# B's factor moved into C, B turned by DMA transposes, denominators between v's products

## The chip, the cores and the metric

One core of one Trainium2 chip runs the kernel. The metric is device microseconds of one execution. TensorE multiplies (PE in the profile, PEld its weight loads), VectorE (DVE) does elementwise work and reductions, ScalarE (ACT) copies, scales and exponentials, GpSimd (POOL) a few fills, and SyncE (SP) issues nearly all DMAs, in order.

## What is computed

Two unrelated parts share the launch, each on an input of 2048 x 448 (bf16), and their outputs are put side by side.

```python
# A: a complex diagonal state space, state of 448
Lam_bar = jnp.exp(dt * Lam)
B_bar = ((Lam_bar - 1.0) / Lam)[:, None] * Bmat
Bu = jnp.einsum("bld,pd->blp", x + 0j, B_bar)
# h[t] = Lam_bar * h[t-1] + Bu[t]
y = 2.0 * jnp.einsum("blp,dp->bld", hseq, Cmat).real + x * Dskip
# B: attention, 16 heads of 28; each position sees 8 keys, 2 apart, looking back
qkv = x @ wqkv
logits = q . k[pos - 2*w] * scale      # w = 0..7; -1e9 before the start
out = (softmax(logits) weighted v) @ wo
```

The factor g = (Lam_bar - 1)/Lam stands at each state, between B and C, and commutes with the recurrence, which is diagonal.

## The kernel before, in words

**Part B** first. The input is turned to `xT`, products on TensorE with half-height operands (64 rows) give q, k and v. The method `Ctx.lanes` (L88) writes TensorE's order by hand: it runs two lanes, the upper and lower 64 rows, one product of each per step, and chains the products (L83). The list `weave` puts other work in at given steps: the steps of `qk` (L282) multiply q by shifted k on VectorE (L295, L299) and sum on TensorE (L306); then come `turn` (step 157, L772: the matrix `mats["g"]` and the first softmax's transposes and maxima, L330 and L332), the two `expo` calls (steps 160 and 164: one product L337 that subtracts the maxima, one exponential on ScalarE, L339), and `prepare` (step 200, that is, when the lanes are done; L777). `prepare` makes two power matrices, B's products and `norm` (L343: eight products that sum the exponentials, L345, then the reciprocal L348 and the weights L349 on VectorE). v's products are evicted by ScalarE to `vd` (L239), and copies between partitions fill its halo (`halo`, L223).

After that `pv` (L375) weights v: for each of two halves of the positions and two groups of four, eight products (L389) and seven sums (L392) on VectorE, each 128 x 1792. The result is turned by a DMA transpose (L404; the last by TensorE, L411) and multiplied with wo (L420).

**Part A** runs on TensorE and ScalarE under those products. The state is in 7 blocks of 64 complex numbers, each a block of 128 rows (real over imaginary). The matrices of powers of Lam_bar are made by `mat` (L587, L599) from small numbers in `Scat`, on VectorE, at places given by `put` (L793) between the steps of `pv`. B is loaded by `load_bc` (L461) in its natural layout to `bX`. `setup_b` (L601) multiplies it by the factor's matrix, which also turns it: 28 products (L607), evicted by ScalarE into `Bcat` with 14 casts (two for each block, L609 and L610). Level 1 (`level1`, L637) multiplies `Bcat` by the input `xaT` (L643) for four interleaved positions b = 0..3, adding the power times the position before (L647), evicted by ScalarE (L650, L652). `scan` (L655) doubles over chunks (L673, L676), `ends` (L678) makes the states at chunk ends `G`, and `correct` (L695) adds to the others on VectorE (L700). `setup_c` (L615) turns C with 28 transposes on TensorE (L621), evicted by ScalarE in 7 copies, behind the first scan. `y` (L706) multiplies the states by C (L715) and adds the skip by a diagonal matrix `Dg` (L572, ScalarE; its numbers come from `skip`, L564).

**Order.** The lanes and what they weave are chained on TensorE. The rest is laid out per engine when the kernel is built, by a planner that goes by priority and its own estimates; each engine then takes its instructions in that order, and waits in place. Tiles with the same tag share memory, so `oT` waits for `bX` to be read, and `Ccat` for the weights `wn`. Level 1 has four PSUM buffers ("mm"), the corrections two ("pt"). SyncE's queue at the start: part B's input and weights, B (`load_bc`), A's input in eight DMA transposes (`load_x`, L475), zeros for the halo, wo, C (`load_c`), D, then the halo copies.

Of the kernel before, what the change touches and what calls it, by code (L numbers as in the profile page):

```python
# [11 lines left out]
ALU = mybir.AluOpType  # L12
AX = mybir.AxisListType
f32 = mybir.dt.float32
bf16 = mybir.dt.bfloat16

S = 2048
D = 448
T = 16
NCH = 128  # L20
KT = 4
KP = 112
KA = 128
# [10 lines left out]
NM = 7  # L34
MP = 8
PL = 64
# [7 lines left out]
NPW = len(KPOW)  # L44
# [3 lines left out]
class Ctx:  # L48
# [4 lines left out]
    def consts(self):  # L53
        nc, pool = self.nc, self.pool
        self.ident = pool.tile([NCH, NCH], bf16, name="ident")
        nc.gpsimd.memset(self.ident[:], 0.0)
        nc.gpsimd.affine_select(out=self.ident[:], in_=self.ident[:], compare_op=ALU.not_equal, fill=1.0,
                                base=0, pattern=[[-1, NCH]], channel_multiplier=1)
        self.nident = pool.tile([NCH, NCH], bf16, name="nident")
        nc.gpsimd.memset(self.nident[:], 0.0)  # L60
        nc.gpsimd.affine_select(out=self.nident[:], in_=self.nident[:], compare_op=ALU.not_equal, fill=-1.0,
                                base=0, pattern=[[-1, NCH]], channel_multiplier=1)

        self.spot, self.spot2 = (pool.tile([1, 1], f32, name=f"spot{i}") for i in range(2))
        self.wz = pool.tile([NCH, 4 * NCH], bf16, name="wz")
        nc.vector.memset(self.wz[:], 0.0)
# [364 lines left out]
class PartA:  # L431
# [7 lines left out]
    def consts(self):  # L439
        self.kv = self.pool.tile([NCH, NPW, NM], f32, name="kv")  # L440
        for i, kk in enumerate(KPOW):
            self.nc.gpsimd.memset(self.kv[:, i, :], float(kk))
        self.Bcat = self.pool.tile([KA, KT, NM, NCH], bf16, name="Bcat")
        self.nc.vector.memset(self.Bcat[0:KA - PL, KT - 1], 0.0)
        self.Scat = self.pool.tile([NCH, NPW + 1, 2, MP], bf16, name="Scat")
        self.nc.vector.memset(self.Scat[:], 0.0)

# [11 lines left out]
        nc.sync.dma_start(self.drow[KT - 1:KT], self.A_Dskip[D - KA:D].unsqueeze(0))  # L459

    def load_bc(self):  # L461
        nc, pool = self.nc, self.pool
        self.bX = pool.tile([NCH, NM, D], bf16, name="bX", tag="bX")
        nc.sync.dma_start(self.bX[0:PL], self.A_Bre.rearrange("(m p) d -> p m d", p=PL))
        nc.sync.dma_start(self.bX[PL:NCH], self.A_Bim.rearrange("(m p) d -> p m d", p=PL))

    def load_c(self):
        nc = self.nc
# [43 lines left out]
    def powers(self, sm, big, karg, ang, kf, angr, ex, turned):  # L512
        nc, V, lre, lim = self.nc, self.nc.vector, self.lre, self.lim
        self.cx.order(V.tensor_scalar(kf[:], ang[:], 1.0 / TWO_PI, MAGIC, op0=ALU.mult, op1=ALU.add).ins,
                      turned["V"], "NoSync")
        V.tensor_scalar(kf[:], kf[:], MAGIC, None, op0=ALU.subtract)
        C1 = 6.28125
        C2 = 1.9353071795864769e-03
        V.scalar_tensor_tensor(angr[:], kf[:], -C1, ang[:], op0=ALU.mult, op1=ALU.add)
        reduced = self.reduced = V.scalar_tensor_tensor(angr[:], kf[:], -C2, angr[:], op0=ALU.mult, op1=ALU.add).ins  # L520
        sn, sh, cs = sm("sn", big), sm("sh", big, "kf"), sm("cs", big, "karg")
        self.cx.order(nc.scalar.activation(sn[:], angr[:], ACT.Sin).ins, turned["A"], "NoSync")
        nc.scalar.activation(sh[:], angr[:], ACT.Sin, scale=0.5)
        den, t0, rden = sm("dn"), sm("t0"), sm("rden")
        for o_, l_ in ((den, lre), (t0, lim)):
            self.cx.order(V.tensor_tensor(o_[:], l_, l_, op=ALU.mult).ins, reduced, "NoSync")
        V.tensor_tensor(den[:], den[:], t0[:], op=ALU.add)
        V.reciprocal(rden[:], den[:])
        V.tensor_scalar(rden[:], rden[:], 2.0, None, op0=ALU.mult)
        pw_im = sm("pw_im", big)  # L530
        V.tensor_tensor(pw_im[:], ex[:], sn[:], op=ALU.mult)
        V.tensor_tensor(cs[:], sh[:], sh[:], op=ALU.mult)
        V.tensor_scalar(cs[:], cs[:], -2.0, 1.0, op0=ALU.mult, op1=ALU.add)
        pw_re = sm("pw_re", big)
        V.tensor_tensor(pw_re[:], ex[:], cs[:], op=ALU.mult)
        Scat = self.Scat
        V.tensor_copy(Scat[0:PL, 0:NPW, 0, 0:NM], pw_re[0:PL])
        V.tensor_scalar(Scat[0:PL, 0:NPW, 1, 0:NM], pw_im[0:PL], -1.0, None, op0=ALU.mult)
        V.tensor_copy(Scat[PL:NCH, 0:NPW, 0, 0:NM], pw_im[PL:NCH])
        V.tensor_copy(Scat[PL:NCH, 0:NPW, 1, 0:NM], pw_re[PL:NCH])  # L540
        self.pw_re, self.pw_im, self.rden = pw_re, pw_im, rden
        self.mats = {}
# [55 lines left out]
            self.mats[key] = t_[:].rearrange("p h q m -> p m (h q)")  # L598
        return self.nc.vector.tensor_tensor(t_[:], in0, in1, op=ALU.mult).ins  # L599

    def setup_b(self, eng):  # L601
        nc, cx = self.nc, self.cx
        def step(i):
            pt, out = cx.ps([KA, KT, NCH], f32, "pt_b"), []
            for k in range(KT):
                c0 = min(k * KA, D - KA)
                out.append(nc.tensor.matmul(pt[:, k, :], lhsT=self.bX[:, i, c0:c0 + KA], rhs=self.mats["g"][:, i, :],  # L607
                                            start=(k == 0), stop=(k == KT - 1), skip_group_check=True).ins)
            cx.ev(eng, self.Bcat[:, 0:KT - 1, i, :], pt[:, 0:KT - 1])  # L609
            cx.ev(eng, self.Bcat[PL:KA, KT - 1, i, :], pt[PL:KA, KT - 1])  # L610
            return out

        return [lambda i=i: step(i) for i in range(NM)]

    def setup_c(self, eng):  # L615
        nc, cx, pool = self.nc, self.cx, self.pool
        self.C = pool.tile([NCH, NM, D], bf16, name="Ccat", tag="wn")
        for m in range(NM):
            pt = cx.ps([NCH, KT, KP], bf16, "pt_c", "pt")
            for a in range(KT):  # L620
                nc.tensor.transpose(pt[:, a, :], self.cn[:, a, m].rearrange("p r q -> p (r q)"), cx.ident[0:KP, 0:KP])  # L621
            cx.ev(eng, self.C[:, m, :].rearrange("p (a q) -> p a q", q=KP), pt[:])

    def alloc_h(self):
        pool = self.pool
# [11 lines left out]
    def level1(self, mh):  # L637
        nc, cx = self.nc, self.cx
        for b in range(4):
            for m in range(*MH[mh]):  # L640
                ps = cx.ps([NCH, 4 * NCH], f32, "l1", "mm")
                for k in range(KT):
                    nc.tensor.matmul(ps[:], lhsT=self.Bcat[:, k, m, :],  # L643
                                     rhs=self.xT[:, b, k, :],
                                     start=(k == 0), stop=(b == 0 and k == KT - 1))
                if b:
                    nc.tensor.matmul(ps[:], lhsT=self.mats[1][:, m, :], rhs=self.h[b - 1][:, m, :],  # L647
                                     start=False, stop=True)
                if b < 3:
                    nc.scalar.copy(self.h[b][:, m, :], ps[:])  # L650
                else:
                    nc.scalar.copy(self.h[b][:, m, :].rearrange("p (a c) -> p a c", a=4),  # L652
                                   ps[:].rearrange("p (c a) -> p a c", a=4))
# [70 lines left out]
def body(ctx: ExitStack, tc: tile.TileContext, A_x, A_Lre, A_Lim, A_Bre, A_Bim, A_Cre, A_Cim, A_logdt, A_Dskip,  # L724
         B_x, B_wqkv, B_wo, out):
    nc = tc.nc
    pool = ctx.enter_context(tc.tile_pool(name="sb", bufs=1))
    psum = ctx.enter_context(tc.tile_pool(name="ps", bufs=1, space=bass.MemoryType.PSUM))
    out_v = out[0].rearrange("(p j) e -> p j e", j=T)
    cx = Ctx(tc, pool, psum)  # L730
    b = PartB(cx, B_x, B_wqkv, B_wo, out_v[:, :, D:2 * D])
    a = PartA(cx, A_x, A_Lre, A_Lim, A_Bre, A_Bim, A_Cre, A_Cim, A_logdt, A_Dskip, out[0].rearrange("(n b) e -> n b e", b=4)[:, :, 0:D])
# [14 lines left out]
    b.load_w(2 * D, 2 * D, D, nc.sync)  # L747
    a.load_bc()
    a.load_x()
    b.zero_halo(b.vd)  # L750
    b.load_wo()
    a.load_c()
# [9 lines left out]
    def later():  # L762
        powers(b.turned)
        b.mix_w(a.reduced)
        a.params_g()
        return ()

    values = [b.proj(j, "A") for j in (*range(HJ, T), *range(HJ))]
    qk, soft = b.qk(0) + b.qk(1), {}
    weave = [(5, turns[2:] + [later])] + [(s_, [f]) for s_, f in zip(WEAVE, qk)]  # L770
# [5 lines left out]

    def prepare():  # L777
        a.mats_behind([0, 3], b.maxima)
        fs = mats_b[:1] + soft[1][0][4:] + mats_b[1:]
        return [ins for f in fs for ins in f()]  # L780

    mats_b = a.setup_b("A")
    weave += [(157, [turn])] + [(160 + 4 * i, [lambda i=i: soft[1][0][2 + i]()]) for i in range(2)] + [(200, [prepare])]
    cx.lanes([b.proj_t(t0, t1, g, "A") for t0, t1, gs in ((0, 256, (0, 1, 2)), (256, 512, (0, 1, 2)), (0, 512, (4, 5, 6, 3)))
              for g in gs]
             + [b.proj_t(*t, g, "A") for t in parts for g in (0, 1, 2, 4, 5, 6, 3)] + values, weave, 10)
    at1 = soft[1][1]
    b.halo(b.vd, 6, HALO)
    b.halo(b.vd, 0, 6)
    a.skip()  # L790
    fs, at0 = b.softmax(0)

# [20 lines left out]
    for b_, r in itertools.product((3, 0, 1, 2), range(4)):  # L813
        ins = a.y(r, b_)
        if (b_, r) == (1, 3):
            wo[2]()
    turn, out = wo[3]
# [35 lines left out]
```

## Time and profile before

| | |
|---|---|
| median of 3 runs | 151.69 us (151.14 to 152.08) |
| the profiled execution | 151.38 us, its span 149.7 us |
| granted TensorE clock | 1.00 throughout |
| DVE, 50 to 60 us | 7.58 us busy |
| DVE, 60 to 100 us | 10.00 us busy in each 10 us |
| PE, 60 to 70 us | 7.93 us busy |
| PE, 70 to 130 us | 9.79 to 10.00 us busy in each 10 us |
| ACT, 50 to 60 us | 8.08 us busy |

Times in a timeline are microseconds from the start of the span. A timeline line gives start, length (for several instructions from the first's start to the last's end), engine, source line, operation, output and inputs, count, and in brackets the idle time before it and what ended it. In the chain that ended last each piece starts where the one before it ends. "SPq" is an issue on SyncE's queue. A mean of busy time hides stages with different limits, so the text goes by the lines in the order of time.

### The profile page before, as it was taken

What the parts mean: (1) busy time and instruction counts of PE and PEld (TensorE: products, weight loads), DVE (VectorE), ACT (ScalarE), POOL (GpSimd) and SP (SyncE); (2) the same over time, 40 slices, a digit from 0 to 9 for tenths busy, and PEclk for the clock granted to TensorE, in tenths of its full rate; (3) what the DMA queues carried; (4) which work ended last, traced back from release to release, by engine and by line L of the source; (5) the groups of instructions that cost most, each with busy time, mean ns of one, the idle gap of its engine ahead of it and who ended that gap; (6) DMA issues with size and microseconds to landing.
All of it is one profiled execution on the core that took longest, in us unless ns stands there. A gap on an engine that the chain in (4) does not pass through costs nothing.

```text
span 149.7 us, 3246 instructions
## 1 busy us (share of the span) xinstructions
PE 139.7 (93%) x1234; PEld 80.6 (54%) x1240; DVE 131.5 (88%) x178; ACT 90.7 (61%) x200; POOL 8.7 (6%) x84
## 2 busy tenths in 40 slices
PE   6999999999999999589999999999999999899790
PEld 2477744445665675245467555568565655445440
DVE  4368999998999859999999999995999999999821
ACT  3387947886754599964569967779421242245340
POOL 8110100000000200000000000000000000000000
PEclk9999999999999999999999999999999999999999
DMA  4999999993767706000004200045111121832121
GB/s 118 286 176 192 176 242 212 95 211 74 144 115 136 213 4 183 0 0 4 0 0 83 39 4 0 0 118 134 61 64 61 41 87 56 190 120 96 61 92 61
DMA packets 35534, 14.77 MB, mean 99 GB/s; under 512 B 27635, under 2 KB 35137, under 8 KB 35519
## 3 DMA queue, kind: packets, MB, share of 16 engines
q1 hardware_dynamic: 34954, 14.12, 44.2%
q10 hardware_dynamic: 565, 0.46, 0.9%
q8 instruction: 9, 0.15, 0.4%
q14 instruction: 6, 0.05, 0.2%
HBM read 3.85 MB, written 3.67 MB: 50 GB/s over the span
## 4 chain that ended last, share of the span: by engine, by line
PE 68%; DVE 18%; ACT 9%; issue 2%; DMA 1%; DVEq 0%; ACTq 0%
PE qk_ps L121 14%; PE l L643 13%; PE v_ps L121 8%; DVE pvb L392 8%; DVE pvb L389 7%; PE lg L306 6%; PE wo_ps L420 5%; PE warm L71 3%; PE y_ps L715 3%; PE l L647 3%; PE gt L690 3%; PE co L699 3%; ACT h L650 2%; PE l L673 2%; ACT Ccat L144 2%
## 5 line engine op out<-in xcount | busy, mean ns | idle before, releaser
L389 DVE TENSOR_TENSOR pvb<-attn,vd 128x1792 bf16<-128x1792 bf16 (+1 forms) x33 | 34.0, 1052 | 0.0
L643 PE MATMUL l<-xaT,Bcat 128*128 128x512 bf16 x108 | 29.5, 379 | 1.8 <-ACT h L650 1.6
L392 DVE TENSOR_TENSOR pvb<-pvb 128x1792 bf16<-128x1792 bf16 (+1 forms) x29 | 30.3, 1049 | 0.0
L295 DVE TENSOR_TENSOR pr<-q,kT 128x3072 bf16<-128x3072 bf16 x16 | 27.9, 1755 | 1.4 <-PE lg L306 0.7
L121 PE MATMUL qk_ps<-xbT,wqkv_nat 64*128 64x512 bf16 (+1 forms) x189 | 24.8, 353 | 0.1
L718 ACT CAST ya<-y_ps 128x448 bf16<-128x448 f32 x16 | 8.4, 533 | 18.7 <-PE y_ps L715 13.0
L715 PE MATMUL y_ps<-Ccat,h 128*128 128x448 bf16 x84 | 18.0, 353 | 0.0
L643 PEld LDWEIGHTS <-Bcat 128*128 128x128 bf16 x112 | 10.5, 99 | 10.7 <-issue 2.2
L121 PEld LDWEIGHTS <-wqkv_nat 64*128 64x128 bf16 x189 | 11.5, 94 | 8.7 <-issue 2.5
L420 PE MATMUL wo_ps<-wo_p,oT 128*128 128x448 bf16 x64 | 14.7, 352 | 1.0 <-DMA oT<-pvb 1.0
L650 ACT CAST h<-l 128x512 bf16<-128x512 f32 x21 | 12.4, 623 | 4.3 <-PE l L647 4.2
L700 DVE TENSOR_TENSOR h<-co,h 128x512 bf16<-128x512 f32 x21 | 13.2, 685 | 2.0 <-PE gt L690 1.6
L121 PE MATMUL v_ps<-wqkv_nat,xbT 64*128 64x448 bf16 x112 | 13.2, 360 | 0.0
L144 ACT CAST kT<-qk_ps 128x512 bf16<-128x512 f32 (+4 forms) x26 | 10.0, 424 | 3.7 <-PE qk_ps L121 3.6
L144 ACT CAST yb<-wo_ps 128x448 bf16<-128x448 f32 x14 | 7.5, 534 | 6.0 <-PE wo_ps L420 3.1
L144 ACT CAST q<-qk_ps 128x512 bf16<-128x512 f32 (+1 forms) x20 | 9.6, 497 | 1.2 <-PE qk_ps L121 1.1
L144 ACT CAST vd<-v_ps 128x448 bf16<-128x448 f32 x16 | 8.0, 539 | 4.0 <-PE v_ps L121 3.8
L715 PEld LDWEIGHTS <-h 128*128 128x128 bf16 x84 | 7.3, 98 | 5.3
L676 ACT CAST pbuf<-l 128x512 bf16<-128x512 f32 (+2 forms) x21 | 9.1, 439 | 1.5 <-PE l L673 1.5
L306 PE MATMUL lg<-pr,ones 128*32 128x256 bf16 x256 | 9.9, 275 | 0.0
L121 PEld LDWEIGHTS <-xbT 64*128 64x128 bf16 x112 | 7.6, 145 | 3.5 <-issue 1.9
L420 PEld LDWEIGHTS <-oT 128*128 128x128 bf16 x64 | 6.0, 98 | 6.5 <-DMA oT<-pvb 1.4
(137 smaller groups left out, 192.0 us busy)
## 6 DMA issues: line engine op xcount, KB each, us to landing
out_dram<-yb SPq DMA_DIRECT2D x16, 112.0 KB, 2.1
out_dram<-ya SPq DMA_DIRECT2D x16, 112.0 KB, 1.7
vd<-vd SPq DMA_DIRECT2D x1, 784.0 KB, 5.4
wqkv_nat<-in_B_wqkv_dram SPq DMA_DIRECT2D x2, 336.0 KB
vd<-vd SPq DMA_DIRECT2D x1, 588.0 KB
xn<-in_B_x_dram SPq DMA_DIRECT2D x2, 224.0 KB, 3.4
bX<-in_A_B_re_dram SPq DMA_DIRECT2D x1, 392.0 KB, 4.4
bX<-in_A_B_im_dram SPq DMA_DIRECT2D x1, 392.0 KB
```

Source lines behind the costliest of these rows:

```text
L121: ins = mm(g["ps"], lhsT=l_, rhs=r_, start=first, stop=not (g["left"][0] or g["left"][1]), skip_group_check=True).ins
L144: nc.scalar.copy(out, in_)
L295: queued(V.tensor_tensor(pr[:], q[0][:, :, n * qu:n * qu + n].unsqueeze(2).to_broadcast([KA, KT - 1, 4, n]), self.shifted(i, 0, KT - 1, s, ...
L306: out.append(mm(lg[32 * t:32 * t + 32, n * qu:n * qu + n], lhsT=l_, rhs=r_, start=not (s or qu or c), stop=(s == 1 and c == KT - 1), skip_ ...
L389: V.tensor_tensor(t_[:, c0:c1], at[:, w, jl0 + c0:jl0 + c1, :].unsqueeze(2).to_broadcast([NCH, c1 - c0, DH, H]), self.vd[:, off + c0:off + ...
L392: ins = V.tensor_tensor(acc[:, c0:c1], acc[:, c0:c1], t_[:, c0:c1], op=ALU.add).ins
L420: ins = nc.tensor.matmul(ps[:], lhsT=oT[:, 7 * i + 3 * odd + k, :], rhs=self.wo_p[:, odd, k, :], start=(k == 0), stop=(k == KT - 1)).ins
L643: nc.tensor.matmul(ps[:], lhsT=self.Bcat[:, k, m, :], rhs=self.xT[:, b, k, :], start=(k == 0), stop=(b == 0 and k == KT - 1))
L650: nc.scalar.copy(self.h[b][:, m, :], ps[:])
L676: nc.scalar.copy(dst[:, :, PAD:], ps[:])
L700: nc.vector.tensor_tensor(self.h[b][:, m, :], ps[:], self.h[b][:, m, :], op=ALU.add)
L715: out.append(nc.tensor.matmul(ps[:], lhsT=self.state(m, r, b), rhs=self.C[:, m, :], start=False, stop=(m == NM - 1), skip_group_check=True ...
```

## The change

B is loaded in the same natural layout, but padded to 512 columns (the last 64 of the 448 stand behind 64 columns of zeros), in four transfers instead of two, and two DMA transposes (`turn_b`) turn it into `Bcat`, whose two middle dimensions change places. The factor is no longer in it. C is turned by one DMA transpose (`turn_c`), and seven products with the factor's matrix (`setup_c`) give what `y` reads. The signs in `Scat` follow. In `prepare`, at step 167 instead of 200, stand the two power matrices and `norm`; the second `expo` stands at step 162 instead of 164. `setup_b` is gone.

```diff
--- before.py
+++ after.py
@@ -440,8 +440,9 @@
         self.kv = self.pool.tile([NCH, NPW, NM], f32, name="kv")
         for i, kk in enumerate(KPOW):
             self.nc.gpsimd.memset(self.kv[:, i, :], float(kk))
-        self.Bcat = self.pool.tile([KA, KT, NM, NCH], bf16, name="Bcat")
-        self.nc.vector.memset(self.Bcat[0:KA - PL, KT - 1], 0.0)
+        self.Bcat = self.pool.tile([KA, NM, KT, NCH], bf16, name="Bcat")
+        self.bX = self.pool.tile([NCH, NM, KT * KA], bf16, name="bX", tag="bX")
+        self.nc.vector.memset(self.bX[:, :, (KT - 1) * KA:KT * KA - PL], 0.0)
         self.Scat = self.pool.tile([NCH, NPW + 1, 2, MP], bf16, name="Scat")
         self.nc.vector.memset(self.Scat[:], 0.0)
 
@@ -459,10 +460,24 @@
         nc.sync.dma_start(self.drow[KT - 1:KT], self.A_Dskip[D - KA:D].unsqueeze(0))
 
     def load_bc(self):
-        nc, pool = self.nc, self.pool
-        self.bX = pool.tile([NCH, NM, D], bf16, name="bX", tag="bX")
-        nc.sync.dma_start(self.bX[0:PL], self.A_Bre.rearrange("(m p) d -> p m d", p=PL))
-        nc.sync.dma_start(self.bX[PL:NCH], self.A_Bim.rearrange("(m p) d -> p m d", p=PL))
+        n = (KT - 1) * KA
+        for r, src in enumerate((self.A_Bre, self.A_Bim)):
+            v, o_ = src.rearrange("(m p) d -> p m d", p=PL), self.bX[r * PL:(r + 1) * PL]
+            self.nc.sync.dma_start(o_[:, :, 0:n], v[:, :, 0:n])
+            self.nc.sync.dma_start(o_[:, :, KT * KA - PL:], v[:, :, n:])
+
+    def turn_b(self):
+
+        for m0, m1 in ((0, 4), (4, 7)):
+            self.nc.sync.dma_start_transpose(self.Bcat[:, m0:m1].rearrange("p m k c -> p (m k) c"),
+                                             self.bX[:, m0:m1].rearrange("p m d -> p (m d)"))
+
+    def turn_c(self):
+        both = self.pool.tile([NCH, 2, NM * D], bf16, name="Ccat", tag="wn")
+        self.C = both[:, 0].rearrange("p (m d) -> p m d", d=D)
+        self.cT = both[:, 1].rearrange("p (a m q) -> p a m q", a=KT, q=KP)
+        self.nc.sync.dma_start_transpose(both[:, 1].rearrange("p (c q) -> p c q", q=KP),
+                                         self.cn[:].rearrange("p a m r q -> p (a m r q)"))
 
     def load_c(self):
         nc = self.nc
@@ -535,8 +550,8 @@
         V.tensor_tensor(pw_re[:], ex[:], cs[:], op=ALU.mult)
         Scat = self.Scat
         V.tensor_copy(Scat[0:PL, 0:NPW, 0, 0:NM], pw_re[0:PL])
-        V.tensor_scalar(Scat[0:PL, 0:NPW, 1, 0:NM], pw_im[0:PL], -1.0, None, op0=ALU.mult)
-        V.tensor_copy(Scat[PL:NCH, 0:NPW, 0, 0:NM], pw_im[PL:NCH])
+        V.tensor_copy(Scat[0:PL, 0:NPW, 1, 0:NM], pw_im[0:PL])
+        V.tensor_scalar(Scat[PL:NCH, 0:NPW, 0, 0:NM], pw_im[PL:NCH], -1.0, None, op0=ALU.mult)
         V.tensor_copy(Scat[PL:NCH, 0:NPW, 1, 0:NM], pw_re[PL:NCH])
         self.pw_re, self.pw_im, self.rden = pw_re, pw_im, rden
         self.mats = {}
@@ -598,28 +613,12 @@
             self.mats[key] = t_[:].rearrange("p h q m -> p m (h q)")
         return self.nc.vector.tensor_tensor(t_[:], in0, in1, op=ALU.mult).ins
 
-    def setup_b(self, eng):
-        nc, cx = self.nc, self.cx
-        def step(i):
-            pt, out = cx.ps([KA, KT, NCH], f32, "pt_b"), []
-            for k in range(KT):
-                c0 = min(k * KA, D - KA)
-                out.append(nc.tensor.matmul(pt[:, k, :], lhsT=self.bX[:, i, c0:c0 + KA], rhs=self.mats["g"][:, i, :],
-                                            start=(k == 0), stop=(k == KT - 1), skip_group_check=True).ins)
-            cx.ev(eng, self.Bcat[:, 0:KT - 1, i, :], pt[:, 0:KT - 1])
-            cx.ev(eng, self.Bcat[PL:KA, KT - 1, i, :], pt[PL:KA, KT - 1])
-            return out
-
-        return [lambda i=i: step(i) for i in range(NM)]
-
     def setup_c(self, eng):
-        nc, cx, pool = self.nc, self.cx, self.pool
-        self.C = pool.tile([NCH, NM, D], bf16, name="Ccat", tag="wn")
+
         for m in range(NM):
-            pt = cx.ps([NCH, KT, KP], bf16, "pt_c", "pt")
-            for a in range(KT):
-                nc.tensor.transpose(pt[:, a, :], self.cn[:, a, m].rearrange("p r q -> p (r q)"), cx.ident[0:KP, 0:KP])
-            cx.ev(eng, self.C[:, m, :].rearrange("p (a q) -> p a q", q=KP), pt[:])
+            ps = self.cx.ps([NCH, D], f32, "c_ps", "pt")
+            self.nc.tensor.matmul(ps[:], lhsT=self.mats["g"][:, m, :], rhs=self.cT[:, :, m, :], start=True, stop=True)
+            self.cx.ev(eng, self.C[:, m, :], ps[:])
 
     def alloc_h(self):
         pool = self.pool
@@ -640,7 +639,7 @@
             for m in range(*MH[mh]):
                 ps = cx.ps([NCH, 4 * NCH], f32, "l1", "mm")
                 for k in range(KT):
-                    nc.tensor.matmul(ps[:], lhsT=self.Bcat[:, k, m, :],
+                    nc.tensor.matmul(ps[:], lhsT=self.Bcat[:, m, k, :],
                                      rhs=self.xT[:, b, k, :],
                                      start=(k == 0), stop=(b == 0 and k == KT - 1))
                 if b:
@@ -747,6 +746,7 @@
     b.load_w(2 * D, 2 * D, D, nc.sync)
     a.load_bc()
     a.load_x()
+    a.turn_b()
     b.zero_halo(b.vd)
     b.load_wo()
     a.load_c()
@@ -776,17 +776,16 @@
 
     def prepare():
         a.mats_behind([0, 3], b.maxima)
-        fs = mats_b[:1] + soft[1][0][4:] + mats_b[1:]
-        return [ins for f in fs for ins in f()]
-
-    mats_b = a.setup_b("A")
-    weave += [(157, [turn])] + [(160 + 4 * i, [lambda i=i: soft[1][0][2 + i]()]) for i in range(2)] + [(200, [prepare])]
+        return soft[1][0][4]()
+
+    weave += [(157, [turn])] + [(160 + 2 * i, [lambda i=i: soft[1][0][2 + i]()]) for i in range(2)] + [(167, [prepare])]
     cx.lanes([b.proj_t(t0, t1, g, "A") for t0, t1, gs in ((0, 256, (0, 1, 2)), (256, 512, (0, 1, 2)), (0, 512, (4, 5, 6, 3)))
               for g in gs]
              + [b.proj_t(*t, g, "A") for t in parts for g in (0, 1, 2, 4, 5, 6, 3)] + values, weave, 10)
     at1 = soft[1][1]
     b.halo(b.vd, 6, HALO)
     b.halo(b.vd, 0, 6)
+    a.turn_c()
     a.skip()
     fs, at0 = b.softmax(0)
```

## The prediction

> **What bounds the kernel now.** I read the page's busy shares first, then the chain that ended last, then VectorE's timeline over the whole span, and last the timelines of ScalarE, TensorE and SyncE around the lines that the diff touches.
>
> ```profile
> PE 139.7 (93%) x1234; PEld 80.6 (54%) x1240; DVE 131.5 (88%) x178; ACT 90.7 (61%) x200; POOL 8.7 (6%) x84
> ```
>
> Two engines are nearly full, so the share decides nothing; the place of the idle time does. VectorE's timeline (start, length, instruction, idle before it):
>
> ```profile
> 54.81 0.96 DVE L348 RECIPROCAL rec<-den 128x128 bf16<-128x128 f32 x1 [1.73 <-PE den L345]
> ...
> 101.90 1.08 DVE L389 TENSOR_TENSOR pvb<-attn,vd 128x1792 bf16<-128x1792 bf16 x1
> 104.57 1.29 DVE L700 TENSOR_TENSOR h<-co,h 128x512 bf16<-128x512 f32 x2 [1.59 <-PE gt L690]
> 106.14 12.04 DVE L700 TENSOR_TENSOR h<-co,h 128x512 bf16<-128x512 f32 x19 [0.28 <-PE co L699]
> ```
>
> From 54.81 to its last product at about 141.3 VectorE rests only 1.59 and 0.28 us, and before that it waits 1.73 us for the denominators. After it comes a tail of transposes and output of some 8.4 us. So the end moves by what those three rests lose, as long as TensorE keeps up. TensorE's part of the chain, where the change bites:
>
> ```profile
> 52.76 0.32 PE lt L337
> 53.08 0.91 PE v_ps L121 x6
> 53.99 0.33 PE pt_b L607 x4
> 54.32 0.45 PE den L345 x8
> 54.77 1.34 PE pt_b L607 x24
> ...
> 59.49 0.47 ACT Bcat L144
> 60.28 0.28 issue
> 60.55 0.97 ACT Dg L572 x3
> 61.55 0.58 ACT h L650
> ```
>
> The reader sees that B's products hand the chain to ScalarE, which then holds it up to the first eviction of level 1. The same in the timeline of all engines:
>
> ```profile
> 54.79 5.44 ACT L144 CAST Bcat<-pt_b 128x384 bf16<-128x384 f32 x14
> ...
> 60.25 1.28 ACT L572 ACTIVATE Dg<-ident,dsk 128x128 bf16<-128x128 bf16 x4
> 61.55 0.58 ACT L650 CAST h<-l 128x512 bf16<-128x512 f32 x1
> ...
> 62.19 1.02 PE L643 MATMUL l<-xaT,Bcat 128*128 128x512 bf16 x4 [1.60 <-ACT h L650]
> ```
>
> ScalarE takes its instructions in order: 14 evictions of Bcat, 4 of Dg, and only then h. TensorE's four buffers for level 1 are full meanwhile, and the second round (b=1) starts at 62.19. From there TensorE is nearly dense to the first correction product at 104.37, whose result ends VectorE's 1.59 us rest. That links ScalarE's 5.44 us to the end.
>
> **The change part by part.**
>
> *B's products leave.* 24 of them stand between 54.61 and 56.04, 0.06 us each, so 28 are 1.7 us of TensorE; 14 evictions are 5.44 us of ScalarE, in the one stretch where ScalarE leads. Nothing on VectorE leaves but a fill of 0.43 us at 1.23, which a smaller fill replaces, ahead of a rest of 2.3 us: nothing. The sign moved between two small instructions (L538, L539, 0.23 and 0.25 us) costs nothing.
>
> *B's transposes come, on SyncE's queue.* Nearest rows, a transpose between two places on chip and its reader:
>
> ```profile
> 127.26 1.52 SPq L404 DMA_TRANSPOSE oT<-pvb  x1
> ...
> 131.27 3.22 PE L420 MATMUL wo_ps<-wo_p,oT 128*128 128x448 bf16 x16 [0.96 <-DMA oT<-pvb]
> ```
>
> It turns 14 blocks: 1.52 us of the queue and 4.0 us to the reader. B has 16 and 12 blocks: 3.0 us of the queue. The two loads of B become four; the old took 0.76 and 0.62 us to issue, so 1.4 us more. SyncE ended the last transpose of A's input at 32.2; the new ones are issued at about 33.6 to 36.6 and land by 41 to 45 (4 to 8 us, if the second waits for the first). Level 1 reads Bcat at 55, so 10 us cover it. What stands behind on the queue slips by 4.4 us: halo zeros, ten transfers of wo, eight loads of C, two of D, the first halo copy. C's last load goes out before 50.5 and lands (3.8) by 54.3. The first halo goes from 47.14 to 51.5, lands by 57 (5.4) and is first read by the product for w=5, the second of the pair at 66.62. The second halo waits 6.2 us for v's last eviction, so it has slack for 4.4. The 10 us cover all of it; without cover each us would be a us of level 1.
>
> *C.* 28 transposes on TensorE (eight from 77.45 to 77.85, so 0.05 us each, 1.4 us) become 7 products of 448 columns. The row of y's products, seven in 1.49 us with a tail, gives 0.19 us each, 1.3 us. Seven copies of 0.59 us become seven casts like ya's, 0.53 us. Nothing either way. The transpose of C is 28 blocks, so twice the row above: 3.0 us of queue and at most 8 us to land. It stands behind the second halo (55.5 to 56.4, both halves out) and needs the weights' buffer, free when v's products end near 55; it lands by 65. The products for C stand at 77.45 now, near 75 then. Behind it on the queue is the transpose at 79.59, with 15 us of cover.
>
> *Denominators.* They were called after all of v's products; now at step 167. Counting the lanes' two products a step, the last step is 167 with a single product, which agrees with the trace (8 products between the two L337, 7 behind the second). The second L337 moves from step 164 to 162. New order, from the first L337's end at 51.85: 4 products 0.46, L337 0.32, 10 products 1.14, then the denominators. The 0.33 us of the chain's four B products less 4 x 0.06 leaves 0.09 for the change of product shape, and 0.45 follow: end 54.31 for 54.77. The exponentials that they read must be there: ScalarE started the second at 53.47 behind two evictions of v whose groups end in steps 162 and 163, now behind it. It can start at 52.7 and end by 53.4, before 53.77. So the reciprocal starts 0.4 us earlier, at 54.4. Ends of this: 0 (if ScalarE keeps its order) and 0.86 (if the products start at 53.4); the rows put it in the middle, and I take 0.4. Queued behind the denominators on TensorE are one product of v, whose eviction ends near 55.4 instead of 54.95 (read by VectorE at 57), and the transposes for softmax.
>
> [...] The row: TensorE's weight loads for L337 show 0.32 us of "issue" behind v's half-height products. [...] The denominators now have such products on both sides, so one pair of changes more. [...]
>
> *TensorE to the first correction.* Denominators end 54.3, one product with its changes 0.6: 54.9. Eight transposes for softmax 0.68, sixteen products of level 1 at 0.215 are 3.44, one L337 0.32: b=1 can start at 59.3, against 62.19. ScalarE has Dg from 56.2 to 57.5 and the first h at 58.0, so it no longer holds. What is late next: L337 for the other softmax needs VectorE's maxima, which end at 59.29 now, 58.9 then; TensorE reaches its place (behind 11 products) at 57.95, so up to 0.95 us is lost again. The gain is 2.0 to 2.9 us. Later, the scan's power 512 comes off VectorE at 83.1, 82.7 then; its products at 85.27 come to 82.4 to 83.3: up to 0.3 us. So the first correction product is at 101.5 to 102.7 instead of 104.37.
>
> *VectorE.* It ends its product at 102.98, then at 102.58, and the correction can follow at 101.7 to 102.9 (0.2 behind its product). The rest of 1.59 us goes, but for 0.3 at the worst. The 0.28 us (wo's products queued ahead of the second pair) I leave in place. TensorE must be earlier at the end too: it rests 0.96 us at 131.27 and 0.87 us at 140.88 there, so 2 us follow.
>
> *Sum.* 0.4 + 1.6 = 2.0 us. The profiled execution took 151.38 us (span 149.7), so 149.4; it lies 0.3 under the median of 151.69, which gives 149.7. I say 149.5.
>
> **The rivals.**
> 1. *The gap stays.* TensorE's order is laid out anew and gives the 2 to 2.9 us back between 59 and 102 (waits for maxima and powers). For it: VectorE is full, and TensorE's margin at the correction is only 0 to 0.9 us. Against: the removed work is in the stretch with 2 us of rest. Then only the 0.4 remains: 151.0, or 151.3 by the median.
> 2. *Slower: TensorE waits for C's transpose.* The new wait is in order. If the layout puts C's products as soon as it believes them ready, near 58, TensorE stands to 65: 7 us, less 2.0 to 2.9. The first correction then comes near 109, and VectorE rests about 6 instead of 1.59: +4.5 less 0.4, 155.5. It costs more than nothing from a wait of 2.4 to 3.3 us on (TensorE's gain and the 0.4), and a per cent from 4 to 5. Against: they were laid at 77.45 though C lay ready from 50, and no transpose here took over 5 us to land.
> 3. *The denominators wait.* If ScalarE keeps two evictions ahead of the second exponential, TensorE stands still up to 0.3 us among v's products and the 0.4 is gone, the rest not: 149.8.
> 4. *More.* The 0.28 and all of 0.86 go as well: 151.38 - 2.73 = 148.65.
>
> **How the numbers follow.** A measurement here tells about 1% from no change: under 150.2 is faster, over 153.2 slower. The forecast with rivals 3 and 4 (148.6 to 150.1): 0.62. Rival 1 (150.2 to 151.7): 0.22. Rival 2, or Bcat late by over 4 us: 0.16. The range reaches from rival 4 with 0.2 for the runs' spread, 148.4, to rival 1's middle, 151.5; what is left out is rival 2 and little else.
>
> **What would show it.** Right: the reciprocal near 54.4; no Bcat casts; h's first eviction near 58; the second round of level 1 near 59 to 60; no rest ahead of the first L700, at about 102.6; SyncE's first halo copy near 51.5. Wrong: a TensorE wait for cT or Bcat, a rest ahead of L700 of a us or more, or TensorE instead of VectorE ending last before the tail.

## The result and the profile after

| | before | after |
|---|---|---|
| median | 151.41 us (151.09 to 152.08) | 149.32 us (149.12 to 149.71) |
| ratio | 1 | 0.9859 (95% interval 0.9814 to 0.9904) |
| profiled execution | 151.38 us, span 149.7 | 149.53 us, span 147.8 |

Two later measurements of the same changed kernel gave 149.9 and 149.53 us against 151.13 and 151.15 (below). So the change gains 1.0 to 1.4%. A ratio leaves out the few executions that took over 1.5% more than the fastest of their kernel, at a mean granted clock of 0.95 to 0.99; a median here is over all of them. The first row of the page after:

```profile
PE 138.3 (94%) x1191; PEld 78.1 (53%) x1191; DVE 131.1 (89%) x178; ACT 85.8 (58%) x186; POOL 8.6 (6%) x84
```

ScalarE (ACT) lost 4.9 us of work and TensorE 1.4, VectorE next to nothing. VectorE's timeline, the lines that answer to those before:

```profile
54.41 0.96 DVE L348 RECIPROCAL rec<-den 128x128 bf16<-128x128 f32 x1 [1.31 <-PE den L345]
...
100.60 1.08 DVE L392 TENSOR_TENSOR pvb<-pvb 128x1792 bf16<-128x1792 bf16 x1
101.60 1.28 DVE L699 TENSOR_TENSOR h<-co,h 128x512 bf16<-128x512 f32 x2
103.16 11.97 DVE L699 TENSOR_TENSOR h<-co,h 128x512 bf16<-128x512 f32 x19 [0.28 <-PE co L698]
```

The rest of 1.59 us ahead of the corrections is gone (no bracket at 101.60); the 0.28 stayed. The wait ahead of the reciprocal is 1.31 for 1.73. The timeline of all engines where B's evictions stood:

```profile
54.74 3.68 SPq L479 DMA_TRANSPOSE Ccat<-cn  x1
54.75 1.25 PE L642 MATMUL l<-xaT,Bcat 128*128 128x512 bf16 x5
...
55.83 0.59 ACT L649 CAST h<-l 128x512 bf16<-128x512 f32 x1 [0.54 <-PE l L642]
...
56.31 1.28 ACT L587 ACTIVATE Dg<-ident,dsk 128x128 bf16<-128x128 bf16 x4
...
60.07 0.38 PE L646 MATMUL l<-h,mat 128*128 128x512 bf16 x1
```

Level 1 starts at 54.75. ScalarE waits for TensorE now and not the other way round. The second round, which began at 62.19, has its first power product (L646; L647 in the kernel before) at 60.07 against 63.05.

Spans of two profiles do not start at quite the same point of the work, so below I also give a length inside VectorE's order: from the first softmax maxima (50.59 before, 50.61 after) to the end of the last sum (141.36 and 139.31). It is 90.77 us before and 88.70 after, 2.07 less.

### The profile page after: what moved, and what is told of

It reads as the page before. It is cut to its first block, busy times and chain, and to the rows that moved or that the text cites. A ratio compares the mean times of both kernels' runs of the same rounds, so it can differ in the third digit from the quotient of the medians.

```text
span 147.8 us, 3145 instructions
## 1 busy us (share of the span) xinstructions
PE 138.3 (94%) x1191; PEld 78.1 (53%) x1191; DVE 131.1 (89%) x178; ACT 85.8 (58%) x186; POOL 8.6 (6%) x84
## 4 chain that ended last, share of the span: by engine, by line
PE 56%; DVE 37%; ACT 2%; issue 2%; DMA 1%; DVEq 0%
DVE pvb L389 15%; PE qk_ps L121 15%; DVE pvb L392 13%; PE v_ps L121 8%; PE lg L306 6%; PE wo_ps L420 5%; PE l L642 5%; PE warm L71 3%; DVE mat L614 3%; PE gt L689 3%; PE y_ps L714 2%; PE co L698 2%; DVE h L699 2%; PE l L672 2%; DMA out_dram<-yb 1%
## 5 line engine op out<-in xcount | busy, mean ns | idle before, releaser
L389 DVE TENSOR_TENSOR pvb<-attn,vd 128x1792 bf16<-128x1792 bf16 (+1 forms) x33 | 33.9, 1053 | 0.0
```

The source lines that it names most:

```text
L389: V.tensor_tensor(t_[:, c0:c1], at[:, w, jl0 + c0:jl0 + c1, :].unsqueeze(2).to_broadcast([NCH, c1 - c0, DH, H]), self.vd[:, off + c0:off + ...
```

## The experiments

The theory: ScalarE's 14 evictions held level 1; without them TensorE reaches the first correction early enough for VectorE to go on without a rest (1.6 us), and the denominators' place gives 0.4 us. Rivals: TensorE's 28 products carry the gain; the denominators carry it; C's shorter way carries it; B's transposes have no real cover.

**The denominators alone**, in the kernel before:

```diff
     def prepare():
         a.mats_behind([0, 3], b.maxima)
-        fs = mats_b[:1] + soft[1][0][4:] + mats_b[1:]
-        return [ins for f in fs for ins in f()]
+        return soft[1][0][4]()
+    def products():
+        return [ins for f in mats_b for ins in f()]
-    weave += ... (160 + 4 * i, ...) ... [(200, [prepare])]
+    weave += ... (160 + 2 * i, ...) ... [(167, [prepare]), (200, [products])]
```

> The kernel before, with the denominators alone moved between v's products; B's 28 products and 14 evictions stay, behind them. My theory: VectorE starts its dense stretch 0.4 us earlier, but the first correction still waits for level 1, which hangs on ScalarE's evictions, so the rest of 1.59 us ahead of it grows to about 2.0 and the time stays: 151.4, ratio 1.000 (0.997 to 1.003). Rival, the denominators carry the gain: 0.4 us or more, ratio 0.997 or less, with the rest ahead of the corrections unchanged.

Measured: 151.03 against 151.14 us, ratio 0.9999 (0.997 to 1.0027). VectorE's timeline:

```profile
54.27 0.96 DVE L348 RECIPROCAL rec<-den 128x128 bf16<-128x128 f32 x1 [1.31 <-PE den L345]
...
104.33 13.39 DVE L700 TENSOR_TENSOR h<-co,h 128x512 bf16<-128x512 f32 x21 [1.80 <-PE co L699]
```

The wait ahead of the reciprocal is the shorter one, and the rest ahead of the corrections grew from 1.59 to 1.80 us: VectorE gives part of what it wins at the start back there, since level 1 sets when the corrections can begin. The 0.28 behind it is gone in this order, and the length inside VectorE's order is 90.44 us, 0.33 less than before. The times don't show that (0.9999, give or take 0.3%, which is 0.4 us). So the denominators alone give 0 to 0.4 us, not the 2.

**The denominators back**, in the changed kernel:

```diff
-    weave += ... (160 + 2 * i, ...) ... [(167, [prepare])]
+    weave += ... (160 + 4 * i, ...) ... [(200, [prepare])]
```

> The changed kernel with the denominators put back behind v's products. My theory: the reciprocal comes 0.4 us later than in the changed kernel, VectorE stays dense to the end, so 149.7 us, ratio 0.989 (0.986 to 0.991). Rival, the denominators' place is what the change gains by: 151.4, ratio 1.000. A second rival, it is worth nothing once B's products are gone, since nothing then stands ahead of the denominators: 149.3, ratio 0.986, reciprocal at 54.4.

Measured: 149.27 us, ratio 0.9869 (0.9847 to 0.9891), which lies among the changed kernel's three ratios. The time is that of the second rival and not my theory's 149.7, though the interval still holds the theory's 0.989. But the reciprocal does wait longer, as my theory said and the rival did not:

```profile
54.40 0.96 DVE L348 RECIPROCAL rec<-den 128x128 bf16<-128x128 f32 x1 [1.70 <-PE den L345]
55.28 0.10 DVE L584 CAST dsk<-pt_d 128x4 f32<-128x4 bf16 x1
55.47 0.69 DVE L349 TENSOR_TENSOR attn<-e,rec 128x1024 bf16<-128x1024 bf16 x1
56.07 0.68 DVE L332 TENSOR_REDUCE mx<-lt 128x64 bf16<-128x512 f32 x1
56.67 2.08 DVE L389 TENSOR_TENSOR pvb<-attn,vd 128x1792 bf16<-128x1792 bf16 x2
```

This profile begins 0.40 us earlier (its first maxima are at 50.21), so the reciprocal is 4.19 us behind them, against 3.80 in the changed kernel. But the first weighted product (L389) is 6.46 us behind, against 6.29: of the 0.4, 0.17 are left. The next maxima (L332) stand ahead of that product in VectorE's new order, and they need TensorE's transposes L330, which stand behind the first products of level 1 and come no earlier with the denominators: from the weights' product (L349) to these maxima it is 0.82 us in the changed kernel and 0.60 here. The length inside VectorE's order is 88.84 us, 0.14 more than the changed kernel's, which the times do not resolve.

**ScalarE's evictions put back**, in the changed kernel, with 4 of the 28 products:

```diff
+    def extra():
+        pt, out = cx.ps([KA, KT, NCH], f32, "pt_b"), []
+        for k in range(KT):
+            out.append(nc.tensor.matmul(pt[:, k, :], lhsT=a.bX[:, 0, k * KA:(k + 1) * KA], rhs=a.mats["g"][:, 0, :], ...).ins)
+        dump = pool.tile([KA, KT, NCH], bf16, name="dump")
+        for i in range(NM):
+            cx.ev("A", dump[:, 0:KT - 1], pt[:, 0:KT - 1])
+            cx.ev("A", dump[PL:KA, KT - 1], pt[PL:KA, KT - 1])
+        return out
-    weave += ... [(167, [prepare])]
+    weave += ... [(167, [prepare]), (200, [extra])]
```

> The changed kernel, with 14 evictions like Bcat's put back on ScalarE (from one PSUM tile, into memory that nobody reads) and only 4 of B's 28 products. My theory, ScalarE's 5.44 us hold level 1: the first eviction of h returns to about 61, the second round of level 1 starts near 61.5 with a TensorE rest of 2 us, the first correction near 103.2, VectorE rests about 1 us ahead of it: 150.3 to 150.9, ratio 0.993 to 0.997. Rival, TensorE's removed products carry the gain: 149.4 to 149.6.

Measured: 152.41 us in the median of twelve (150.88 to 155.4), ratio 1.0045 (1.0014 to 1.0076), both above what I expected; the profiled execution, at a granted clock of 1.00, took 151.0 us. The whole gain is gone. Timeline of ScalarE and TensorE, then VectorE's:

```profile
54.79 5.50 ACT L144 CAST dump<-pt_b 128x384 bf16<-128x384 f32 x14
60.31 1.28 ACT L587 ACTIVATE Dg<-ident,dsk 128x128 bf16<-128x128 bf16 x4
61.61 1.17 ACT L339 ACTIVATE e<-lt 128x512 bf16<-128x512 f32 x2
62.67 2.54 ACT L649 CAST h<-l 128x512 bf16<-128x512 f32 x5
```

```profile
61.39 0.54 PE L620 MATMUL c_ps<-Ccat,matg 128*128 128x448 bf16 x2 [2.36 <-DMA Ccat<-cn]
...
63.30 1.02 PE L642 MATMUL l<-xaT,Bcat 128*128 128x512 bf16 x4
```

```profile
103.81 1.29 DVE L699 TENSOR_TENSOR h<-co,h 128x512 bf16<-128x512 f32 x2 [1.62 <-ACT G L691]
105.58 11.98 DVE L699 TENSOR_TENSOR h<-co,h 128x512 bf16<-128x512 f32 x19 [0.48 <-PE co L698]
```

The rest is back, 1.62 us, and the mechanism is the expected one. The length inside VectorE's order is 90.52 us, 1.82 more than the changed kernel's. The planner changed two more things: both exponentials of the other softmax (L339) now stand ahead of h on ScalarE, and TensorE's order has C's products early, where it waits 2.36 us for their transpose. The exponentials put h back by 1.1 us (61.61 to 62.67). The wait for C shows no cost of its own: ScalarE has no idle time from 54.79 to h at 62.67, and level 1's next product starts at 63.30, when that h is done and long after the wait has ended at 61.39. So this run shows that the evictions suffice to take the gain, not that they cost just that much.

**TensorE's products put back**, without evictions:

```diff
+    def extra():
+        out = []
+        for i in range(NM):
+            pt = cx.ps([KA, KT, NCH], f32, "pt_b")
+            for k in range(KT):
+                out.append(nc.tensor.matmul(pt[:, k, :], lhsT=a.bX[:, i, k * KA:(k + 1) * KA], rhs=a.mats["g"][:, i, :], ...).ins)
+        return out
-    weave += ... [(167, [prepare])]
+    weave += ... [(167, [prepare]), (200, [extra])]
```

> The changed kernel, with B's 28 products put back on TensorE at their old place and no evictions (their results are not read). My theory: 1.7 us more of TensorE ahead of level 1, which was dense to the first correction (101.1), so this comes at 102.8; VectorE fills part of it with a product that stands behind the corrections, and rests 0.2 to 0.8 us: 149.5 to 150.1, ratio 0.988 to 0.992. Rival, only ScalarE's evictions count: 149.3, no rest. Rival, only the products count: 150.9.

Measured: 148.68 us, ratio 0.9835 (0.9811 to 0.9859): nothing lost against the changed kernel's 0.986 to 0.990. Timelines of TensorE and VectorE:

```profile
54.46 1.74 PE L786 MATMUL pt_b<-matg,bX 128*128 128x128 bf16 x28
...
101.84 0.60 PE L698 MATMUL co<-G,mat 128*128 128x512 bf16 x2
...
102.39 13.12 DVE L699 TENSOR_TENSOR h<-co,h 128x512 bf16<-128x512 f32 x21
```

The products took 1.74 us, but the first correction came only 0.9 us later than in the changed kernel (101.84 for 100.94; 1.1 us counted from the first maxima). VectorE did one more sum or product ahead of the corrections and then ran all 21 without a rest: the 0.28 us is gone too, and the length is 88.26 us, 0.44 less than the changed kernel's. So the products were hidden in this order, and the rival that only the evictions count was right; I had given the products 0.2 to 0.8 us.

This run and the first one, measured side by side, make the cleanest pair. Both have B's 28 products and the early denominators, and the first has the evictions and no transposes of B and C by DMA: 151.03 against 148.68 us, length 90.44 against 88.26. No wait for C's transpose stands in either.

**C turned by TensorE as before:**

```diff
-        self.nc.sync.dma_start_transpose(both[:, 1].rearrange("p (c q) -> p c q", q=KP), ...)
...
-            ps = self.cx.ps([NCH, D], f32, "c_ps", "pt")
-            self.nc.tensor.matmul(ps[:], lhsT=self.mats["g"][:, m, :], rhs=self.cT[:, :, m, :], start=True, stop=True)
-            self.cx.ev(eng, self.C[:, m, :], ps[:])
+            pt = self.cx.ps([NCH, KT, KP], bf16, "pt_c", "pt")
+            for a in range(KT):
+                self.nc.tensor.transpose(pt[:, a, :], self.cn[:, a, m].rearrange("p r q -> p (r q)"), ...)
+            self.cx.ev(eng, self.C[:, m, :].rearrange("p (a q) -> p a q", q=KP), pt[:])
```

> The changed kernel, with C turned by 28 transposes on TensorE as before, and no DMA transpose of C; this leaves the factor g out of the computation. My theory, C's way costs the same either way (1.4 us of transposes against 1.3 us of products): ratio 0.986 (0.984 to 0.989). Rival, C's shorter work on TensorE is part of the gain: 149.6 or more.

Measured: 149.66 us, ratio 0.9898 (0.9857 to 0.9938); the changed kernel, measured side by side, 149.9 us and 0.9899 (0.9867 to 0.993). The rival's 149.6 is reached, but by the changed kernel too. C's way costs the same either way, as far as the times resolve. Lengths inside VectorE's order agree: 88.68 and, in the changed kernel's first profile, 88.70 us.

**The changed kernel again**, twice:

> The changed kernel again, on the same chip as the others of this call: 149.3 us, ratio 0.986 (0.983 to 0.989).

> The changed kernel once more, on the chip of this call: 149.3 to 149.9 us, ratio 0.986 to 0.990.

Measured: 149.9 us, ratio 0.9899 (0.9867 to 0.993), and 149.53 us, ratio 0.9874 (0.9844 to 0.9904). The first of the two left a profile of 150.13 us that shows two things which the other two profiles of the changed kernel do not. TensorE's timeline:

```profile
54.79 0.09 PEld L582 LDWEIGHTS <-drow 4*128 4x128 bf16 x1 [0.94 <-DMA drow<-in_A_Dskip_dram]
...
130.34 4.89 PE L420 MATMUL wo_ps<-wo_p,oT 128*128 128x448 bf16 x16 [1.98 <-DMA oT<-pvb]
```

First, TensorE waits 0.94 us for D, whose load stands near the end of SyncE's longer queue (issued at 52.68); VectorE then rests 0.24 and 0.66 us. Second, 16 products took 4.89 us for 3.22, at a granted clock near 0.50 for 3 us of them (last section), and behind them TensorE, not VectorE, sets the end. Its product that turns VectorE's last result, first in the changed kernel's first profile, then in this one:

```profile
138.83 0.56 PE L411 MATMUL pt_o<-ident,pvb 128*128 128x128 bf16 x7 [1.05 <-DVE pvb L392]
```

```profile
139.44 0.55 PE L411 MATMUL pt_o<-ident,pvb 128*128 128x128 bf16 x7
```

In the first TensorE waits for VectorE's last sums. In the second it comes late and doesn't wait, and the span runs 8.9 us beyond VectorE's last sum for 8.5.

**D's loads early** (every other engine's order stays the same):

```diff
+    a.load_d()
     a.load_bc()
...
     a.load_c()
-    a.load_d()
```

> The changed kernel, with D's two loads moved ahead of B's on SyncE's queue; every other engine's order is the same. In one profile of the changed kernel TensorE waits 0.94 us for D's load, which the longer queue has pushed to 53.5, and VectorE then 0.24 and 0.66 us; in the other it does not. My theory, this wait is a new one that the change made, and it comes and goes: no wait of TensorE for D here, 148.9 to 149.3 us, 0.3 to 0.9 us under the changed kernel of this call. Rival, the spread of the changed kernel has another source (TensorE's granted clock near 131 us): no difference over 0.2 us.

Measured: 149.54 us, ratio 0.9879 (0.985 to 0.9907), beside 149.53 for the changed kernel, measured side by side. No difference, so this theory of the spread is not borne out. But the changed kernel's profile there has no wait for D, so the run can't tell how often the wait comes; that is left open. Where the wait is there, it counts: the profile with it has 89.44 us inside VectorE's order, 0.7 more than the first. The rival, the granted clock near 131 us, is in part borne out: it lengthens the end by 0.5 us in that profile, and by 0.8 in the profile of the run that follows (last section).

**B's transposes late.** First behind C's in the program:

```diff
-    a.turn_b()
...
     b.halo(b.vd, 0, 6)
+    a.turn_b()
     a.turn_c()
```

> The changed kernel, with B's two transposes behind the transpose of C on SyncE's queue, where they wait for the end of v's products: issued near 58.5 to 63, landing 62 to 67 instead of 41, against level 1 that could start at 54.8. My theory, no cover and each us is one of level 1: the first product of level 1 near 62 to 64, the first correction 7 to 9 us later, VectorE rests 6 to 8 us less the one product it can take ahead: 155 to 158 us, ratio 1.025 to 1.045. Rival, the planner fills TensorE with other work and level 1 has slack: under 151.

Measured: 149.44 us, ratio 0.9877 (0.9846 to 0.9909). The run was not the one that I meant, since the planner issued the transposes ahead of the halo copies. SyncE's queue:

```profile
48.08 4.02 SPq L472 DMA_TRANSPOSE Bcat<-bX  x2
52.21 0.76 SPq L224 DMA_DIRECT2D vd<-vd  x1
```

They were 15 us later than in the changed kernel (32.9). The profile gives 5.5 us from issue to landing for one of the two; for the first that would be 53.6, just ahead of level 1 at 54.3. They cost nothing. The cover in the prediction is real. Then behind both halo copies by force:

```diff
+    self.last_halo = self.nc.sync.dma_start(t_[113:128, r0:r1], ...).ins
...
+            self.cx.order(self.nc.sync.dma_start_transpose(...).ins, after, "NoSync")
...
+    a.turn_b(b.last_halo)
```

> The changed kernel, with B's two transposes ordered behind both halo copies on SyncE's queue, so that they are issued after v's last eviction, near 56 to 59, and land near 60 and 64; level 1 could start at 54.8. It takes the place of the run in which the planner kept them ahead of the halos. My theory, without its cover each us is one of level 1: first product of level 1 near 60.5, 5.7 us late; TensorE is nearly full from there to the end and gets back 1 to 2 us: 152.5 to 154.5 us, ratio 1.01 to 1.023. Rival, level 1 has slack: 149.3 to 150.

Measured: 153.62 us, ratio 1.0131 (1.008 to 1.0182). Its profile is of an execution of 155.84 us, in which the granted clock was 0.50 from 60 to 70 us, so it is used for the order alone. TensorE's timeline:

```profile
59.64 0.90 PE L620 MATMUL c_ps<-Ccat,matg 128*128 128x448 bf16 x2 [2.55 <-DMA Ccat<-cn]
...
65.34 0.61 PE L642 MATMUL l<-xaT,Bcat 128*128 128x512 bf16 x1 [1.08 <-DMA Bcat<-bX]
```

With the cover gone, level 1 waits for Bcat, 10.6 us later than in the changed kernel and not 5.7: B's transposes were issued from 59.59 on. The time is 4.1 us longer in the median (153.62 less 149.53), within what I expected, but for about twice the lateness; so a us of lateness cost less than a us, and part of the 4.1 may be the clock: the mean granted clock of the six executions was 0.95 to 0.99. In this profile TensorE ends last, 3.4 us behind VectorE's last sum (145.13 and 141.77). The wait of TensorE for C's transpose, my slower rival, is here as well (2.55 us), as it was with the evictions put back (2.36): both times the planner had put C's products early.

**A faster version.** The wait of 1.31 us ahead of the reciprocal is idle time of the engine that sets the end, so work was moved into it:

```diff
-        a.mats_behind([0, 3], b.maxima)
+        a.mats_behind([0, 3, 4, 5], b.maxima)
...
-    wo = [b.pv(1, at1, 0, 4, between=[put(4, *fs[:2]), put(5, 6), ...
+    wo = [b.pv(1, at1, 0, 4, between=[put(*fs[:2]), put(6), ...
```

> The changed kernel, with two more power matrices (8 and 12) made on VectorE ahead of the denominators, in the 1.31 us in which it waits for them, and not between the first sums. My theory, VectorE sets the end from the reciprocal on: its dense stretch is two matrices of 0.6 us shorter, the wait falls to about 0.1, TensorE loses its short wait for the power 512 (0.3 us): 148.1 to 148.6 us, ratio to the kernel before 0.979 to 0.982. Rival, TensorE is the bound now and VectorE's time is free: 149.0 to 149.4, with the 1.2 us back as rests of VectorE.

Measured: 147.7 us, ratio 0.9765 (0.9738 to 0.9793), 0.4 us under the range that I gave. The length inside VectorE's order is 87.45 us, 1.25 under the changed kernel's, which is the size expected; TensorE's rest ahead of wo's products is 1.02 us for 1.98, and the granted clock did not fall behind it (0.999 in the mean of that execution, for 0.987 where it fell). Whether that gives the remainder is not shown. With D's loads early as well:

> The kernel with two power matrices made ahead of the denominators, and D's loads early as well. Its profile without the early loads had a TensorE wait of 0.52 us for D and a VectorE rest of 0.46 us behind it. Expected: both gone, 147.1 to 147.5 us, ratio to the kernel before 0.973 to 0.976. Rival, the rest moves elsewhere: 147.7, ratio 0.977.

Measured: 147.53 us, ratio 0.9749 (0.9722 to 0.9775), the fastest here, in the expected range of ratios. Its VectorE timeline:

```profile
51.34 2.49 DVE L614 TENSOR_TENSOR mat<-Dm,Scat 128x1024 bf16<-128x1024 bf16 x4
53.93 0.96 DVE L348 RECIPROCAL rec<-den 128x128 bf16<-128x128 f32 x1
...
100.92 13.15 DVE L699 TENSOR_TENSOR h<-co,h 128x512 bf16<-128x512 f32 x21
```

Four matrices fill the wait, and no bracket is left up to the last sum. The length inside VectorE's order is 87.12 us, 1.6 under the changed kernel: 1.2 from the two matrices, 0.3 from the rest between corrections. Without the early loads the profile has 87.45 us and a rest of 0.46 behind TensorE's wait for D; the times of the two do not tell them apart. The rival that TensorE is the bound after the change is out: VectorE's shorter stretch went through to the time.

## Why the prediction was right, and where its steps were not

- *The sum, 2.0 us.* Measured in the trace 2.07 (length inside VectorE's order), in the medians 2.09, 1.2 and 1.6. The mechanism, ScalarE's evictions holding level 1 and so the corrections, is shown from both sides: put back, they take the gain; the products put back take nothing. VectorE still sets the end in the first profile after, as forecast.
- *The term of 0.4 us for the denominators was mis-sized.* The reciprocal came at 54.41 as forecast, but of the 0.4 only some 0.2 is left where the weighted products begin (0.14 to 0.17 against the run with the denominators back). The step failed where it let everything behind the reciprocal move with it: VectorE's next maxima wait for transposes that TensorE takes behind level 1. Counted from start to start in VectorE's order, the 2.07 is 0.43 from the wait ahead of the reciprocal, less 0.21 at the maxima, 1.64 from the rest ahead of the corrections, and two things that were not in the sum: 0.12 from the cast of D's numbers (L569 before, L584 after), which now falls into the time between the reciprocal and the weights' product, and 0.09 inside the corrections. So it is luck that the sum came out so close: 0.2 too much met 0.2 left out.
- *TensorE's 1.7 us of products.* I counted them in the 2.0 to 2.9 us by which the corrections come earlier. They did come earlier, at 100.94 for 104.37, more than forecast (101.5 to 102.7), but VectorE needed only part of it. The corrections stand one sum or product earlier in VectorE's new order, at 101.60 and not at 102.6. The margin that I put at 0 to 0.9 us was wide enough for the products.
- *The first eviction of h* came at 55.83, ahead of the four casts of Dg, and not at 58.0 behind them as I had it; level 1's second round came near 59 to 60 all the same (its first power product at 60.07).
- *C costs nothing either way:* as forecast. The transposes on SyncE: issued 32.89 to 37.46 (forecast 33.6 to 36.6), the first halo copy at 51.55 (51.5). C's transpose took 3.68 us of queue for 3.0, landed in 5.4, and stood ahead of the second halo copy, not behind it.
- *What the text missed:* D's loads. I listed them among what slips by 4.4 us and covered all with 10 us; TensorE reads D at 54.6, and they were issued at 50.65 and 51.20 in one profile and 52.68 in another. It cost 0.7 us in one execution, and nothing that the times of two kernels side by side could tell. Nor did it have the granted clock of 0.50 behind TensorE's longer rest near 130 us (1.98 us, for 0.96 before), which cost 0.5 us in the same execution.
- *What is late next:* the power 512, as forecast. VectorE's pair at 82.16 ends its first at 82.8, and the scan's product starts at 82.89.
- *The gap at a change of product shape.* In the trace after, the denominators' weight loads show 0.32 us of issue behind v's products, and the chain has 0.55 us for them with that gap, against 0.09 + 0.45 in my sum: the smaller gap was the better number for the path. What makes the gap is not shown.

## What to carry to other kernels

Ask of a removed product what its eviction did on the engine that evicts: here 28 products on a nearly full TensorE were worth nothing, and 14 small evictions, ahead of others on an engine busy 61% of the time, were nearly the whole gain. An instruction that comes 0.4 us earlier is worth 0.4 only if what stands behind it on its engine waits for nothing else; here some 0.2 of it was left. And when one engine is dense up to the end, look for its own idle time ahead of that stretch and move work into it: two small matrices gave another 1.3% (0.9765 against 0.9899, measured side by side), as much as the whole change.

## What the runs showed of the hardware

TensorE's granted clock fell from 1.00 to about 0.50 behind rests of 1.98 and 2.31 us, in some executions only. In the repeated changed kernel, the window from 130 to 135 us (after the first number, the window's length, busy times of PE, PEld, DVE, ACT and POOL, then granted clock, DMA share and GB/s):

```profile
130.00:135.00 5.00, 4.66 (x16) 2.06 (x17) 5.00 (x6) 1.59 (x3) 0.00 (x0) 0.66 0.22 74
```

In windows of 1 us the clock is 0.51, 0.50 and 0.50 from 131 to 134. The rest was 1.98 us there. A rest of 2.31 us in the first run with B's transposes late was followed by the same: 16 products in 4.88 us, and a clock of 0.66 from 130 to 135 us. Rests of 1.98 us in the changed kernel's first profile and of 2.37 us with the denominators back, at the same place, were followed by a clock of 1.00 (16 products in 3.22 and 3.23 us). So the length of the rest alone doesn't decide it, and what does is left open.

The cost was 1.7 us of TensorE (4.89 for 3.22). VectorE shows no rest from it, but TensorE then reaches its last transposes late: the span ends 8.9 and 9.2 us behind VectorE's last sum in these two profiles, and 8.4 to 8.5 in the two others. So it cost 0.5 and 0.8 us of time.
